# A block-wise attention and a sine-gated MLP in one Trainium2 kernel: the first load goes ahead of an index table, and work units, PSUM banks and a weight load are dealt anew

## The chip, the core and the metric

The kernel runs on one core of a Trainium2 chip. A core has a matrix engine (TensorE, PE in the profile, with weight loads shown as PEld), a vector engine (VectorE, DVE), a scalar engine for functions and copies (ScalarE, ACT), a general engine (GpSimd, POOL) and a queue engine (SyncE, SP). Each takes its own instructions in order. Data comes and goes by 16 DMA engines; a load that converts float32 to bf16 on its way is issued by POOL. The metric is the device time of one execution in microseconds. The median of three runs of the kernel before is 210.96 us (210.64 to 211.02).

## The reference

Two operators in a row. The first is a linear attention over 4 batches, 8 heads, 768 positions and 64 channels with a decay `lam` per head, written in blocks of 64; the second is an MLP on the 3072 x 512 result.

```python
for b in range(nb):                                  # blocks of 64 positions
    intra = einsum('bhic,bhjc->bhij', qb, kb) * Dmask    # lam^(i-j), i >= j
    intra = einsum('bhij,bhjd->bhid', intra, vb)
    inter = einsum('bhid,bhde->bhie', qb * lam_pow, kv_state)
    out[:, :, sl] = intra + inter
    kv_state = lam_block * kv_state + einsum('bhsd,bhse->bhde', kb * rev_pow, vb)
x = out.transpose(0, 2, 1, 3).reshape(3072, 512)
h = x @ w_in                                         # 512 x 2048
g = h + sin(alpha * h)**2 / (alpha + 1e-9)
result = g @ w_out                                   # 2048 x 512
```

## The kernel before, in words

The 768 positions are cut into six chunks of 128 (`NT`), and a chunk holds all four batches, so the MLP works on 512 rows at a time. While PE does the MLP of chunk g, the attention of chunk g+1 is laced into it.

**Loads.** k and q of chunk 0, batch 0, come as float32 from SP and ACT (L81). All others are issued by POOL in program order: `load` (L104, and L101 and L102 where heads are turned by one), `load_w_in` (L89), `load_w_out` (L92). In the program's order they are: k and q of batches 1 to 3, v in two halves, w_in in four quarters (the first in two halves), w_out's first quarter (L544), and then, between POOL's own work on decayed keys (`decay_k`, tile `kdec`, L226) and on the mask table (`mask_table`, L189), the loads of chunk 1 and the other quarters of w_out. Before the first of these loads POOL fills `dist`, a table of i - j (`iota`, L110), from which DVE makes the identity, the triangle and the position columns (L125 to L144).

**Chunk 0** (L499 to L554) has a routine of its own. k and q are turned on PE (`turn`, L265) and copied from PSUM by ACT (L267); `scores1` multiplies them (L290) and DVE applies the decay mask (L294, tile `STm`, from the pool `work`, which has three buffers of it); `outs` multiplies with v (L300) and brings the result to `xt`, by ACT for batch 0 (L304) and with the table `Etab` by DVE for the others (L306). ACT makes `Etab` (L183) and, in `decay_tables` (L155, L178), the tables R128, NE64, R64, L128 and L64; L128 is read by nobody. `spin` (L496) issues products of a constant.

**The MLP.** `hidden(g, f)` makes one of 16 blocks of 128 hidden channels: four products of 128x128 by 128x512 into one PSUM bank (L433), then Sin on ACT (L436) and its square on ACT (L441) or DVE (L449). `finish` adds it to h on DVE (L450, tile `gall`). `project(g, m, part)` is the output product, cut into units of four products (L461); a unit needs four finished blocks and one quarter of w_out. `store` copies a finished output tile (ACT L470, DVE L468). Units stand in a list, `behind`, and `run(n)` issues the next n of them. `units` names the places of a chunk's loop at which one is run, and `own` those at which chunk 1's own units join the list.

**Attention of later chunks.** `turns_pair` and `turn` (or a DMA, L242) turn k and q; `states` makes the products of keys and values (L349), `update` adds them to the decayed state on DVE (L327), and POOL casts it to bf16 (L330); `scores` and `masks` (L366, L373) are the products within a block; `outputs_first` multiplies q with the state (L380), `outputs` adds the part within the block (L408), and `leave` scales the sum into `xt` (L415). For chunk 0 the first state comes from `states1` (L316, L324).

**Order and banks.** The order is written out by hand. The eight PSUM banks are also given out by hand: `bank(name, n)`; a new tile in a bank waits until all readers of the one before it are done. `H0` lists the banks of chunk 0's hidden blocks. Between the chunk-0 loop (L581) and the chunk-1 loop (L674) lies a tail (L605 to L635) in which the attention of chunk 1 is interleaved with ten units.

Of the kernel before, what the change touches and what calls it, by code (L numbers as in the profile page):

```python
# [9 lines left out]
ACTF = mybir.ActivationFunctionType  # L10
# [5 lines left out]
def kernel(  # L16
# [29 lines left out]
    qkp = ctx.enter_context(tc.tile_pool(name="qk", bufs=2))  # L46
    vp = ctx.enter_context(tc.tile_pool(name="vv", bufs=3))
    trp = ctx.enter_context(tc.tile_pool(name="trans", bufs=2))
    work = ctx.enter_context(tc.tile_pool(name="work", bufs=3))
    kdp = ctx.enter_context(tc.tile_pool(name="kdec", bufs=2))  # L50
    kvp = ctx.enter_context(tc.tile_pool(name="kvstate", bufs=2))
    xtp = ctx.enter_context(tc.tile_pool(name="xt", bufs=2))
# [5 lines left out]
    def bank(nm, n, dtype=FP32):  # L58
        return psum.tile([P, 512 if dtype is FP32 else 1024], dtype, name=nm, tag=f"b{n}")
# [35 lines left out]
    def load(t, nm, b0, b1):  # L95
# [7 lines left out]
        else:  # L103
# [2 lines left out]
    new_chunk(0)  # L106
    new_chunk(1)

    dist = consts.tile([P, T], FP32, name="dist")
    nc.gpsimd.iota(out=dist[:], pattern=[[1, T]], base=0, channel_multiplier=-1,  # L110
                   allow_small_or_imprecise_dtypes=True)
    for b in range(1, B):
        for nm in "kq":
            load(0, nm, b, b + 1)
    for b in (0, 2):
# [48 lines left out]
    Etab = consts.tile([P, HP, T], FP32, name="Etab")  # L164
    Eb = Etab[:, :, 0:D].unsqueeze(1).broadcast_to([P, 2, HP, D])
    L64 = consts.tile([P, 2, HP], FP32, name="L64")
    L128 = consts.tile([P, 2, HP], FP32, name="L128")
    later = {}

    def decay_tables():  # L170
        nc.scalar.copy(out=lnlam[:, H:H + 2], in_=lnlam[:, 0:2])
        later["R128"] = powers("R128", 2, lnlam[:], [P, H + 2])
        later["NE64"] = powers("NE64", 3, lnlam[:].rearrange("p (hp hd) -> p hd hp", hd=2), [P, 2, HE])
        later["R64"] = powers("R64", 4, lnlam[:], [P, H + 2])
        for L, n in ((L128, T), (L64, D)):
            for pr in range(2):
                for hd, half in enumerate(HALF):
                    nc.scalar.activation(out=L[half, pr, :], in_=lnlam[half, pr + hd:pr + hd + H - 1:2],  # L178
                                         func=ACTF.Exp, scale=float(n))

    def etab(*cs):
        for c in cs:
# [114 lines left out]
    def outs(t, b, n, eng=None):  # L297
        O = bank("O_ps", n)[:].rearrange("p (c i) -> p c i", c=HP)
        for h in range(H):
            nc.tensor.matmul(out=O[halves(h % 2), h // 2, :], lhsT=vn[t][:, b, h, :], rhs=STm[t, b][:, h % 2, h // 2, :],  # L300
                             start=(h < 2), stop=True, skip_group_check=True)
        x = xt[t][:, :, b * T:(b + 1) * T]
        if eng is nc.scalar:
            nc.scalar.copy(out=x, in_=O)  # L304
        else:
            nc.vector.tensor_tensor(out=x, in0=O, in1=Etab[:], op=ALU.mult)  # L306
# [117 lines left out]
            return V if f in (1, 3, 5, 7, 9, 13) else A  # L424
        return A

    H0 = (0, 1, 2, 3, 5, 6, 7, 0, 1, 2, 5, 0, 1, 2, 0, 1)

    def hidden(g, f, between=None):
        hps = bank("hps", H0[f] if g == 0 else (5, 6, 4)[f] if g == 1 and f < 3 else AB[0] if g == 1 and f == 15 else AB[f + 1] if g == 2 and f < 2 else (1, 0, 2)[(f + 2) % 3] if g == 1 and f > 6 else HB[(16 * g + f + 1) % 3])  # L430
        w = w_in_sb[f // 4]
        for c in range(NDC):
            nc.tensor.matmul(out=hps[:], lhsT=w[:, c, (f % 4) * P:(f % 4 + 1) * P],  # L433
                             rhs=xt[g][:, c, :], start=(c == 0), stop=(c == NDC - 1))
        s_sb = mlps.tile([P, GRP], BF16, name="s_sb")
        nc.scalar.activation(out=s_sb[:], in_=hps[:], func=ACTF.Sin, scale=alpha_sb[:, f:f + 1])  # L436
        if between:
            between()
        s2 = mlps.tile([P, GRP], BF16, name="s2")
        if squarer(g, f) is A:  # L440
            nc.scalar.activation(out=s2[:], in_=s_sb[:], func=ACTF.Square)  # L441
        elif squarer(g, f) is G:
            nc.gpsimd.tensor_tensor(out=s2[:], in0=s_sb[:], in1=s_sb[:], op=ALU.mult)
        hps_of[g, f] = (hps, s_sb, s2)
# [10 lines left out]

    def project(g, m, part):
        if part == 0:
            ops_of[g, m] = bank("ops", (OB, AB[3], 1, OB)[m] if g == 0 else AB[0] if g > NT - 3 and m % 2 else OB)
        ops = ops_of[g, m]
        for f in range(4 * part, 4 * part + 4):  # L460
            nc.tensor.matmul(out=ops[:], lhsT=gall[g][:, f, m * P:(m + 1) * P],  # L461
                             rhs=w_out_sb[part][:, f % 4, :],
                             start=(f == 0), stop=(f == NFC - 1))
# [29 lines left out]
    def spin(n, bk, cols=256):  # L493
        ps = bank("hps", bk)
        for _ in range(n):
            nc.tensor.matmul(out=ps[:, 0:cols], lhsT=fill[:, 0:P], rhs=fill[:, 0:cols], start=True, stop=True)  # L496
# [36 lines left out]
    scores1(0, 3, (4, 5))  # L533
    spin(2, 1)
    outs(0, 0, 3, A)
    outs(0, 1, 1)
    warm = consts.tile([P, 1], FP32, name="warm")
    nc.scalar.activation(out=warm[:], in_=lnlam[:, 0:1], func=ACTF.Sin)
    spin(2, 6)
    outs(0, 2, 2)  # L540
    spin(2, 6)
    outs(0, 3, 0)
    spin(5, 6)
    load_w_out(0)  # L544
    decay_k(0, 0, 2)
    for nm in "kq":
        load(1, nm, 0, 2)
    decay_k(0, 2, 4)
    load(1, "v", 0, 2)
    mask_table()  # L550
    load_w_out(1)
    for nm in "kv":
        load(1, nm, 2, 4)
    decay_k(1, 0, 2)  # L554
# [20 lines left out]
    def run(n):  # L575
        for _ in range(min(n, len(behind))):
            behind.pop(0)()
# [2 lines left out]
                    (1, 3), (2, 3), (3, 0), (3, 1), (3, 2), (3, 3)])  # L580
    for f in range(NFC):  # L581
        hidden(0, f)
        if f in (6, 9):
            states1(0, f // 3 - 2, 4 + 2 * (f == 9))
        if f == 9:
            load_w_out(2)
            load(1, "q", 2, 4)
            load_w_out(3)
        if f in (11, 12):
            run(1)  # L590
        if f == 12:
            turns_pair(1, "k", 0, 6, (A, A))
        if f == 13:
            turn(1, "q", 0, 4, A)
            turn(1, "q", 1, 5, V)
        if f == 14:
            scores(1, (0,), (5, 6))
            masks(1, 0)
        if f == 15:
            states(1, (0,), (4, 2))  # L600
            update(1, 0, 0)
            finish(0, 14)
        if f != 14:
            finish(0, f)
    decay_k(1, 2, 4)  # L605
    load(2, "v", 0, 2)
    update(1, 1, 0)
    run(2)
    turns_pair(1, "k", 2, 0, (A, A))
    outputs_first(1, (0,), (5, 6), A)  # L610
    load(2, "v", 2, 4)
    run(1)
    outputs(1, (0,))
    leave(1, 0, (0,))
    run(1)
    states(1, (1,), (4, 2))
    update(1, 0, 1)
    leave(1, 0, (1,))
    load(2, "k", 0, 2)
    run(2)  # L620
    turn(1, "q", 2, 0, A)
    turn(1, "q", 3, 4, V)
    run(1)
    scores(1, (1,), (0, 5))
    masks(1, 1)
    load(2, "k", 2, 4)
    outputs_first(1, (1,), (6, 4), A)
    update(1, 1, 1)
    load(2, "q", 0, 2)
    load(2, "q", 2, 4)  # L630
    run(1)
    outputs(1, (1,))
    leave(1, 1)
    run(2)
    pair_ready(2, 0)  # L635


# [36 lines left out]
    for g in range(1, NT + 1):  # L674
        if g < NT:
            gall[g] = gbp.tile([P, NFC, GRP], BF16, name="gall")
        at = slots(g) if g + 1 < NT else {}
        fd = feed(g) if g + 1 < NT else {}
        if g + 1 < NT:
            new_xt(g + 1)  # L680
        own = {9: (0, 0), 10: (0, 1), 14: (0, 2)} if g == 1 else {}
        units = [1, 3, 5, 6, 9, 10, 14] if g == 1 else [i for i in range(NFC) if g > 2 or i not in (0, 2, 3)]
        for i in range(NFC):
            if g == NT and not behind:
                break
# [46 lines left out]
```

## Time and profile before

| | |
|---|---|
| median of three runs | 210.96 us |
| the profiled execution | 210.92 us |
| its span (first to last recorded instruction) | 209.1 us |
| granted TensorE clock | 1.0 |
| PE busy | 197.3 us, 94% |
| ACT busy | 144.4 us, 69% |
| DVE busy | 135.3 us, 65% |
| POOL busy | 93.6 us, 45% |
| first product of chunk 0's MLP | 17.31 us |
| first product of chunk 1's MLP | 49.60 us |
| last output copy | 205.83 us |

The tables of the profile are read so. In the chain of waits a line gives start, length, engine and the tile or source line. In a timeline a line gives start, length, engine, line, operation, what is written from what is read, and in brackets the idle time of that engine just before, with what ended it. In a table of stretches a line gives the stretch, its length, each engine's busy time with the number of instructions, the granted clock, the DMA share (mean packets in flight for a DMA engine times the length) and GB/s.

### The profile page before, as it was taken

What the parts mean: (1) busy time and instruction counts of PE and PEld (TensorE: products, weight loads), DVE (VectorE), ACT (ScalarE), POOL (GpSimd) and SP (SyncE); (2) the same over time, 40 slices, a digit from 0 to 9 for tenths busy, and PEclk for the clock granted to TensorE, in tenths of its full rate; (3) what the DMA queues carried; (4) which work ended last, traced back from release to release, by engine and by line L of the source; (5) the groups of instructions that cost most, each with busy time, mean ns of one, the idle gap of its engine ahead of it and who ended that gap; (6) DMA issues with size and microseconds to landing.
All of it is one profiled execution on the core that took longest, in us unless ns stands there. A gap on an engine that the chain in (4) does not pass through costs nothing.

```text
span 209.1 us, 5355 instructions
## 1 busy us (share of the span) xinstructions
PE 197.3 (94%) x2203; PEld 97.7 (47%) x2233; DVE 135.3 (65%) x260; ACT 144.4 (69%) x242; POOL 93.6 (45%) x99
## 2 busy tenths in 40 slices
PE   6679998999989999999999999999999999999993
PEld 2444445554444544445444444445444444444462
DVE  4674997665599878978548978557867544444000
ACT  4699999216988898765776775776675787887121
POOL 8999949897639941998942207002000000000000
PEclk9999999999999999999999999999999999999999
DMA  5999999999999999999999908601101101110212
GB/s 103 155 159 206 205 164 181 182 180 155 159 268 71 147 147 170 91 164 183 142 148 191 183 4 136 168 0 53 50 3 53 50 0 50 52 53 0 100 60 92
DMA packets 98920, 24.47 MB, mean 117 GB/s; under 512 B 91072, under 2 KB 95952, under 8 KB 98896
## 3 DMA queue, kind: packets, MB, share of 16 engines
q0 software_dynamic: 77200, 13.37, 85.2%
q1 hardware_dynamic: 20512, 10.50, 23.8%
q10 hardware_dynamic: 1184, 0.27, 0.6%
q8 instruction: 17, 0.28, 0.5%
q14 instruction: 7, 0.06, 0.1%
HBM read 27.28 MB, written 6.29 MB: 161 GB/s over the span
## 4 chain that ended last, share of the span: by engine, by line
PE 66%; DMA 15%; ACT 5%; POOL 5%; DVE 4%; issue 3%; POOLq 0%; ACTq 0%
PE ops L461 32%; PE hps L433 27%; DMA kn<-in_k_dram 7%; DMA w_out<-in_moe_w_out_dram 5%; DMA qn<-in_q_dram 3%; ACT s_sb L436 2%; DVE S L327 2%; POOL kdec L226 2%; PE hps L485 2%; ACT s L441 2%; PE O_ps L380 2%; DVE gall L450 1%; PE F_ps L366 1%; PE O_ps L408 1%; PE KV_ps L349 1%
## 5 line engine op out<-in xcount | busy, mean ns | idle before, releaser
L450 DVE SCALAR_TENSOR_TENSOR gall<-s,r_sb,hps 128x512 bf16<-128x512 bf16 x96 | 70.8, 744 | 42.1 <-ACT s L441 41.8
L433 PE MATMUL hps<-xt,w_in 128*128 128x512 bf16 x370 | 94.9, 379 | 1.6 <-ACT QKT L282 0.3
L461 PE MATMUL ops<-w_out,gall 128*128 128x512 bf16 x352 | 90.4, 379 | 2.0 <-DMA w_out<-in_moe_w_out_dram 0.7
L436 ACT ACTIVATE s_sb<-hps,alpha_sb 128x512 bf16<-128x512 f32 x96 | 65.4, 685 | 33.6 <-PE hps L433 33.0
L441 ACT ACTIVATE s<-s_sb 128x512 bf16<-128x512 bf16 x90 | 56.7, 630 | 2.9
L433 PEld LDWEIGHTS <-w_in 128*128 128x128 bf16 x384 | 36.6, 98 | 44.0 <-issue 1.5
L461 PEld LDWEIGHTS <-gall 128*128 128x128 bf16 x368 | 35.0, 98 | 41.4 <-issue 1.3
L330 POOL CAST sb<-S 128x512 bf16<-128x512 f32 x20 | 12.2, 617 | 37.5 <-DVE S L327 34.2
L226 POOL TENSOR_TENSOR kdec<-kn,R 128x1024 bf16<-128x1024 bf16 x12 | 22.8, 1908 | 5.2 <-DMA kn<-in_k_dram 4.9
L327 DVE SCALAR_TENSOR_TENSOR S<-S,L,KV_ps 128x128 f32<-128x128 f32 x72 | 20.0, 342 | 0.6 <-PE KV_ps L349 0.6
L415 DVE TENSOR_TENSOR xt<-O_ps,Etab 128x512 bf16<-128x512 f32 x20 | 12.8, 682 | 3.5 <-PE O_ps L408 3.5
L104 POOL DMA_DIRECT2D vn<-in_v_dram x12 | 14.3, 1191 | 0.0
L470 ACT COPY o_sb<-ops 128x512 f32<-128x512 f32 x11 | 6.4, 578 | 10.2 <-PE ops L461 10.2
L373 DVE TENSOR_TENSOR STm<-F_ps,C 128x512 bf16<-128x512 f32 x20 | 12.8, 681 | 0.8 <-PE F_ps L366 0.8
L468 DVE COPY o_sb<-ops 128x512 f32<-128x512 f32 x12 | 8.3, 689 | 4.1 <-PE ops L461 4.1
L267 ACT COPY QKT<-T_ps 128x512 bf16<-128x512 bf16 x10 | 5.7, 586 | 6.4 <-PE T_ps L265 6.4
L398 POOL COPY QKT<-QKT 64x2 bf16<-64x2 bf16 x3 | 0.6, 186 | 19.4 <-PE O_ps L380 11.2
L496 PE MATMUL hps<-fill 128*128 128x256 bf16 (+1 forms) x32 | 7.6, 358 | 1.5 <-DVE fill L123 1.5
L104 POOL DMA_DIRECT2D kn<-in_k_dram x8 | 8.8, 1100 | 0.3 <-issue 0.3
L104 POOL DMA_DIRECT2D qn<-in_q_dram x8 | 8.6, 1077 | 0.0
L380 PEld LDWEIGHTS <-sb 64*64 64x64 bf16 x320 | 4.2, 108 | 4.3 <-issue 4.2
L294 DVE TENSOR_TENSOR STm<-F_ps,C 128x512 bf16<-128x512 f32 x8 | 5.0, 682 | 1.7 <-PE O_ps L300 1.1
(69 smaller groups left out, 109.4 us busy)
## 6 DMA issues: line engine op xcount, KB each, us to landing
out_dram<-o_sb SPq DMA_DIRECT2D x23, 256.0 KB, 2.5
vn<-in_v_dram POOLq DMA_DIRECT2D x12, 256.0 KB, 7.7
w_out<-in_moe_w_out_dram POOLq DMA_DIRECT2D x4, 512.0 KB, 12.5
w_in<-in_moe_w_in_dram POOLq DMA_DIRECT2D x3, 512.0 KB, 12.0
kn<-in_k_dram POOLq DMA_DIRECT2D x5, 256.0 KB, 8.1
qn<-in_q_dram POOLq DMA_DIRECT2D x5, 256.0 KB, 7.8
kn<-in_k_dram POOLq DMA_DIRECT2D x5, 240.0 KB, 8.6
qn<-in_q_dram POOLq DMA_DIRECT2D x5, 240.0 KB, 9.6
```

What stands on the lines that cost most here:

```text
L104: nc.gpsimd.dma_start(out=to, in_=by_head)
L226: nc.gpsimd.tensor_tensor(out=kdec[t][:, b0:b1, :, :], in0=kn[t][:, b0:b1, :, :], in1=R[:, o:o + H].unsqueeze(1).unsqueeze(3).broadcast_to ...
L327: nc.vector.scalar_tensor_tensor(out=S[:, bs, hp, :], in0=old[:, bs, hp, :], scalar=decay[:, pr, hp:hp + 1], in1=ps[:, :, hp, :], op0=ALU. ...
L330: nc.gpsimd.tensor_copy(out=dst[:, bs], in_=S[:, bs])
L373: nc.vector.tensor_tensor(out=st[:, hd], in0=att["F", t, pr, hd], op=ALU.mult, in1=of_mask(C64, t, pr, hd).unsqueeze(1).broadcast_to([P, 2 ...
L380: nc.tensor.matmul(out=att["O", t, pr, blk][halves(h % 2), u, h // 2, :], lhsT=home(t, blk)[halves(half), 2 * pr + m // HP, m % HP, :], rh ...
L415: nc.vector.tensor_tensor(out=xview(t)[:, 2 * pr:2 * pr + 2, blk, :, :], in0=att["O", t, pr, blk], in1=Eb, op=ALU.mult)
L433: nc.tensor.matmul(out=hps[:], lhsT=w[:, c, (f % 4) * P:(f % 4 + 1) * P], rhs=xt[g][:, c, :], start=(c == 0), stop=(c == NDC - 1))
L436: nc.scalar.activation(out=s_sb[:], in_=hps[:], func=ACTF.Sin, scale=alpha_sb[:, f:f + 1])
L441: nc.scalar.activation(out=s2[:], in_=s_sb[:], func=ACTF.Square)
L450: nc.vector.scalar_tensor_tensor(out=gall[g][:, f, :], in0=s2[:], scalar=r_sb[:, f:f + 1], in1=hps[:], op0=ALU.mult, op1=ALU.add)
L461: nc.tensor.matmul(out=ops[:], lhsT=gall[g][:, f, m * P:(m + 1) * P], rhs=w_out_sb[part][:, f % 4, :], start=(f == 0), stop=(f == NFC - 1))
```

## The change

The first load (k of batch 1) is issued before the index table, and q of batch 1 after it. The pool `work` gets a fourth buffer. L128 is dropped, and the tables for blocks of 64 are made after ACT's copy of batch 0. The spins of chunk 0's end are dealt anew (five products in place of nine, most of them ahead of batch 2). The first hidden block is cut by columns into batches 0 to 2 and batch 3. The second quarter of w_out is issued ahead of v of chunk 1. `states1` of the first pair moves from f=6 to f=3. In the tail one unit is run before the states, one after the turned keys, and three in place of two at the end, so that eleven units lie there; chunk 1's loop has six places in place of seven. Banks are renumbered to suit.

```diff
-    work = ctx.enter_context(tc.tile_pool(name="work", bufs=3))
+    work = ctx.enter_context(tc.tile_pool(name="work", bufs=4))
...
+    load(0, "k", 1, 2)
     dist = consts.tile([P, T], FP32, name="dist")
     nc.gpsimd.iota(out=dist[:], pattern=[[1, T]], base=0, channel_multiplier=-1,
                    allow_small_or_imprecise_dtypes=True)
-    for b in range(1, B):
+    load(0, "q", 1, 2)
+    for b in range(2, B):
...
-        for L, n in ((L128, T), (L64, D)):
-            for pr in range(2):
...
-    H0 = (0, 1, 2, 3, 5, 6, 7, 0, 1, 2, 5, 0, 1, 2, 0, 1)
+    H0 = (0, 1, 2, 3, 5, 6, 7, 0, 1, 2, 5, 0, 1, 2, 0, 2)
...
-        for c in range(NDC):
-            nc.tensor.matmul(out=hps[:], lhsT=w[:, c, (f % 4) * P:(f % 4 + 1) * P],
-                             rhs=xt[g][:, c, :], start=(c == 0), stop=(c == NDC - 1))
+        for n0, n1 in ((0, GRP - T), (GRP - T, GRP)) if g + f == 0 else ((0, GRP),):
+            for c in range(NDC):
+                nc.tensor.matmul(out=hps[:, n0:n1], lhsT=w[:, c, (f % 4) * P:(f % 4 + 1) * P],
+                                 rhs=xt[g][:, c, n0:n1], start=(c == 0), stop=(c == NDC - 1))
...
-            ops_of[g, m] = bank("ops", (OB, AB[3], 1, OB)[m] if g == 0 else AB[0] if g > NT - 3 and m % 2 else OB)
+            ops_of[g, m] = bank("ops", (OB, AB[3], 6, OB)[m] if g == 0 else AB[0] if g > NT - 3 and m % 2 else OB)
...
     outs(0, 0, 3, A)
+    decay_tables_64()
     outs(0, 1, 1)
...
-    spin(2, 6)
+    spin(4, 6)
     outs(0, 2, 2)
-    spin(2, 6)
     outs(0, 3, 0)
-    spin(5, 6)
+    spin(1, 6)
...
     decay_k(0, 2, 4)
+    load_w_out(1)
     load(1, "v", 0, 2)
     mask_table()
-    load_w_out(1)
...
-        if f in (6, 9):
-            states1(0, f // 3 - 2, 4 + 2 * (f == 9))
+        if f in (3, 9):
+            states1(0, f // 9, 4 + 2 * (f // 9))
...
         if f == 15:
-            states(1, (0,), (4, 2))
+            run(1)
+            states(1, (0,), (4, 1))
...
-    run(2)
-    turns_pair(1, "k", 2, 0, (A, A))
-    outputs_first(1, (0,), (5, 6), A)
+    run(1)
+    turns_pair(1, "k", 2, 5, (A, A))
+    run(1)
+    outputs_first(1, (0,), (0, 5), A)
     load(2, "v", 2, 4)
     run(1)
     outputs(1, (0,))
     leave(1, 0, (0,))
-    run(1)
-    states(1, (1,), (4, 2))
+    states(1, (1,), (4, 1))
...
-    turn(1, "q", 2, 0, A)
-    turn(1, "q", 3, 4, V)
+    turn(1, "q", 2, 2, A)
+    turn(1, "q", 3, 0, V)
     run(1)
-    scores(1, (1,), (0, 5))
+    scores(1, (1,), (5, 2))
...
-    outputs_first(1, (1,), (6, 4), A)
+    outputs_first(1, (1,), (0, 4), A)
...
     leave(1, 1)
-    run(2)
+    run(3)
...
-        own = {9: (0, 0), 10: (0, 1), 14: (0, 2)} if g == 1 else {}
-        units = [1, 3, 5, 6, 9, 10, 14] if g == 1 else [i for i in range(NFC) if g > 2 or i not in (0, 2, 3)]
+        own = {6: (0, 0), 9: (0, 1), 14: (0, 2)} if g == 1 else {}
+        units = [1, 3, 5, 6, 9, 14] if g == 1 else [i for i in range(NFC) if g > 2 or i not in (0, 2, 3)]
```

More of the change, by code (lines that the diff above doesn't have):

```diff
@@ L166 @@
     L64 = consts.tile([P, 2, HP], FP32, name="L64")
-    L128 = consts.tile([P, 2, HP], FP32, name="L128")
     later = {}
@@ L172, in decay_tables, with decay_tables_64 @@
         later["R128"] = powers("R128", 2, lnlam[:], [P, H + 2])
+    def decay_tables_64():
         later["NE64"] = powers("NE64", 3, lnlam[:].rearrange("p (hp hd) -> p hd hp", hd=2), [P, 2, HE])
         later["R64"] = powers("R64", 4, lnlam[:], [P, H + 2])
-        for L, n in ((L128, T), (L64, D)):
-            for pr in range(2):
-                for hd, half in enumerate(HALF):
-                    nc.scalar.activation(out=L[half, pr, :], in_=lnlam[half, pr + hd:pr + hd + H - 1:2],
-                                         func=ACTF.Exp, scale=float(n))
+        for pr in range(2):
+            for hd, half in enumerate(HALF):
+                nc.scalar.activation(out=L64[half, pr, :], in_=lnlam[half, pr + hd:pr + hd + H - 1:2],
+                                     func=ACTF.Exp, scale=float(D))
     def etab(*cs):
@@ L425, in squarer @@
         return A
-    H0 = (0, 1, 2, 3, 5, 6, 7, 0, 1, 2, 5, 0, 1, 2, 0, 1)
+    H0 = (0, 1, 2, 3, 5, 6, 7, 0, 1, 2, 5, 0, 1, 2, 0, 2)
     def hidden(g, f, between=None):
-        hps = bank("hps", H0[f] if g == 0 else (5, 6, 4)[f] if g == 1 and f < 3 else AB[0] if g == 1 and f == 15 else AB[f + 1] if g == 2 and f < 2 else (1, 0, 2)[(f + 2) % 3] if g == 1 and f > 6 else HB[(16 * g + f + 1) % 3])
+        hps = bank("hps", H0[f] if g == 0 else (5, 7, 4)[f] if g == 1 and f < 3 else AB[0] if g == 1 and f == 15 else AB[f + 1] if g == 2 and f < 2 else (1, 0, 2)[(f + 2) % 3] if g == 1 and f > 6 else HB[(16 * g + f + 1) % 3])
         w = w_in_sb[f // 4]
-        for c in range(NDC):
-            nc.tensor.matmul(out=hps[:], lhsT=w[:, c, (f % 4) * P:(f % 4 + 1) * P],
-                             rhs=xt[g][:, c, :], start=(c == 0), stop=(c == NDC - 1))
+        for n0, n1 in ((0, GRP - T), (GRP - T, GRP)) if g + f == 0 else ((0, GRP),):
+            for c in range(NDC):
+                nc.tensor.matmul(out=hps[:, n0:n1], lhsT=w[:, c, (f % 4) * P:(f % 4 + 1) * P],
+                                 rhs=xt[g][:, c, n0:n1], start=(c == 0), stop=(c == NDC - 1))
         s_sb = mlps.tile([P, GRP], BF16, name="s_sb")
```

## The prediction

> **What bounds it now.** I read the page's busy shares first (PE 94% of the span), then the chain of waits, then the timeline of each stretch, then bytes per stretch. From 49.6 us on, PE goes on almost without a break. So two things can move the end: when PE can begin that stretch, and gaps in it. The chain names the first:
>
> ```profile
> 0.83 0.23 POOL dist L110
> 1.06 0.27 issue
> 1.33 1.08 POOL kn L104
> 2.41 0.89 POOL qn L104
> ...
> 36.03 10.44 DMA w_out<-in_moe_w_out_dram
> 46.47 0.04 issue
> 46.51 0.38 PE ops L461
> ```
>
> The last quarter of w_out lands at 46.47, and PE takes it at 46.51. It is no lone late load. Issue plus time to landing (the tiles' answers) gives: second w_in quarter 10.6 + 10.2 = 20.8; first w_out quarter 12.76 + 15.7 = 28.46; k of chunk 1, batches 0-1, 30.32; second w_out quarter 23.88 + 12.5 = 36.4; k, batches 2-3, 38.0; third w_out quarter 33.45 + 8.8 = 42.25; q, batches 2-3, 43.87. PE is at each within 0.3 us, with one exception (that k pair: turned at 31.30). The timeline shows two of these waits, and POOL issued the loads 9 to 16 us earlier, so their place in line counts and not their issue:
>
> ```profile
> 20.83 0.76 PEld L433 LDWEIGHTS <-w_in 128*128 128x128 bf16 x5 [0.40 <-DMA w_in<-in_moe_w_in_dram]
> 36.42 1.89 PE L461 MATMUL ops<-w_out,gall 128*128 128x512 bf16 x8 [0.50 <-DMA w_out<-in_moe_w_out_dram]
> 42.34 1.89 PE L461 MATMUL ops<-w_out,gall 128*128 128x512 bf16 x7 [0.25 <-DMA w_out<-in_moe_w_out_dram]
> ```
>
> The line never runs dry: 145 to 160 GB/s while it carries q, k, v and 200 to 210 for weights, to 55 us. Only its beginning has room (columns as in the stretches: busy per engine, clock, DMA share, GB/s):
>
> ```profile
> 2.00:3.00 1.00, 1.00 (x4) 0.30 (x3) 0.48 (x4) 0.95 (x1) 1.00 (x2) 1.00 0.26 53
> 3.00:4.00 1.00, 1.00 (x4) 0.32 (x3) 0.00 (x0) 0.04 (x1) 1.00 (x2) 1.00 0.70 155
> 6.00:7.00 1.00, 0.18 (x2) 0.00 (x0) 0.52 (x1) 0.58 (x1) 1.00 (x2) 1.00 2.42 154
> ```
>
> DMA share 0.26 and 0.70 against 2.42 when full: bytes brought into 2 to 4 us shorten all that follows.
>
> **Part by part.** Times are those of the profiled execution (210.92; span 209.1 and 1.82 around it), 0.04 under the median 210.96.
>
> 1. First load ahead of the index table. POOL now runs L110 at 0.83, a gap of 0.27, then k at 1.33. The gap belongs either to the table (k then starts at 0.83: 0.50 earlier) or to the load (1.10: 0.23 earlier). The next load, q, now waits for k and the table: 0.83 + 1.08 + 0.23 + 0.27 = 2.41, as before. Its data landed 5.8 us after issue, so at least 2 us stood in line (a 256 KB v load into an empty line, issued at 63.46, took 4.7) and it loses nothing. The line gains what k can move early: 0 if the two raw loads, in flight until about 6.4, give back what it takes, 0.50 at most. I take 0.4, nearer the upper end because 2 to 4 us was so empty. DVE's work on the table (ten instructions, 1.31 to 2.49) moves about 1.1 later, to 3.6; the first taker is ACT at 5.48, and DVE's next own work is at 4.20. Free; without that cover, up to 1.1 on the first turns.
>
> The ten DVE instructions now lie beside q's issue: 0.90 for a load without them, 1.08 for the one with them. The Trainium skill ("SBUF — State Buffer", section "SBUF: two separate sides") says that VectorE in a two-port mode keeps GpSimd from writing descriptors; the 0.18 agrees. By it q would come 0.18 later, still inside its 2 us in line.
>
> 2. Front. The fourth mask product waited 1.07 for its buffer until O_ps of L300 was done (14.08); with four buffers it can start at about 13.35. The second half of v lands at about 15.25 as before; the spin (0.33) between its two products goes ahead of them. DVE then scales batch 2 at 15.75 and batch 3 at 16.4, done at 17.05 (was 17.16). The first hidden block starts on batches 0-2 at 16.5 instead of 17.31: 4 x 0.16 + 4 x 0.06 (four transposes of 128 columns take 0.23) = 0.88, done at 17.4 instead of 18.17. ACT keeps pace: four L128 instructions go (4 x 0.204), so Sin is loaded 0.8 earlier. That is 0.8 for PE up to f=4, and then PE stands before the w_in quarter of 20.8. Kept: 0. The first states product moves from f=6 to f=3 and lies inside that stand.
>
> 3. w_out ahead of v, and order in the tail. The wait of 0.50 at 36.42 goes. Late next is v: now 32.0 (k, then q at 1.7 per 256 KB) + 2.5 (512 KB at 205) = 34.5 for w_out and 36.2 for v. PE: h of f=15 waits 0.4 for bank 2 (gall of 13, done about 34.65), ends 35.6, its unit 36.4, states just behind v. All that waits for states sits behind it on DVE (four state updates 1.12, then gall 14 and 15), and then POOL's cast (0.62) and kdec (1.90): inter-block products possible at 38.9, kdec at 40.8. PE wants the first at 39.5 (a further 0.4 goes to bank 5, whose two QKT copies end at 39.87) and the second at 41.9. Both hide. PE then stands before the third w_out quarter as now, 42.3. So PE's times against the line are unchanged: 0 kept, 0 lost.
>
> 4. One unit (4 x 0.216 = 0.86) moves ahead of chunk 1, one goes from i=10. PE's sum is the same. States of chunk 2 come 0.86 later relative to the rest, and from there DVE ran without a break from 57.90 to 68.61. That train shifts by 0.86, so h of f=12, which needs bank 2 from f=9's gall, can start at 68.75 (67.83 + 0.86, and its semaphore). It started at 68.74. On the way PE wins 0.42 because the ACT copy of L470 no longer stands before the QKT copies (wait at 62.06), and gives it back at f=12:
>
> ```profile
> 60.76 1.02 PE L433 MATMUL hps<-xt,w_in 128*128 128x512 bf16 x4 [0.28 <-DVE gall L450]
> 62.06 1.02 PE L433 MATMUL hps<-xt,w_in 128*128 128x512 bf16 x4 [0.28 <-ACT QKT L282]
> ```
>
> Bounds: -0.44 if DVE has slack that I don't see, +0.15 if ACT's later block 10 pushes the four x scalings of 70.30. I take 0.
>
> Sum: -0.4 (line) + 0 + 0 + 0: 210.92 - 0.4 = **210.5**.
>
> **Rivals.**
>
> - A, the forecast: the line shifts by 0.2 to 0.5, all else returns to it: 210.4 to 210.7. Chance 0.45.
> - B, the change doesn't do what it says: the line doesn't start earlier. For it: raw loads already moved 270 to 280 GB/s at 4.2 to 5.0, so k's early bytes may only push them back. Against it: share 0.26 and 0.70 before 4.0. Time 210.92 less 0 to 0.2: 210.7 to 210.9. Chance 0.14. The Trainium skill ("DMA: Bandwidth & Descriptors", section "Queues, rings and completion order") says that an engine turns round-robin between its queues by packets, which by itself would make early k packets cost the raw loads turns; the trace of before has no case of it. By that the sum would be 210.9.
> - C, more: the shift is 0.5 and the 0.42 at 62.06 stays won, or the 0.42 at 60.76 goes too: 210.92 - 0.5 - 0.42 = 210.0; 209.9 to 210.4. For it: both waits are in the rows. Against: DVE's unbroken train. Chance 0.27.
> - D, slower: v becomes the late load. Both halves of that swap share 16 engines that finish apart; today no row shows when v landed, only that it was there at 35.48. If it lands 1.2 late, at 37.4, PE stands in order before it, with 0.25 of slack ahead of the k turn (37.8 against 38.06). It decides from 36.6 on. Price 1.2 - 0.25 = 0.95, less 0.4: 211.4 to 211.6. Against it: total bytes ahead of it are the same as those ahead of w_out now. Chance 0.14.
>
> **How the numbers follow.** About 0.2% (0.42) is what a measurement of this kernel can tell from no change, so under 210.54 counts as faster and over 211.38 as slower. A lies across the bound: 0.18 faster, 0.27 same. C is faster (0.27), B the same (0.14), D slower (0.14). Faster 0.45, same 0.41, slower 0.14. Range: C's lower part at 210.0, and upward past B to 211.1, leaving out most of D and a little of C.
>
> **What would show it.** Step 1: k issued at 0.83 to 1.1; third and fourth w_out quarter at PE 0.2 to 0.5 before 42.34 and 46.51. If h of f=0 starts at about 16.5 and the wait on w_in at f=4 grows, step 2 is right; if PE runs on through it, the line came earlier than I think. Step 3: a wait on v in place of the 0.50 on w_out, under 0.3; more is D. Step 4: h of f=12 in chunk 1 starts 22.2 after the fourth w_out quarter is taken (68.74 - 46.51); less is C. The forecast is wrong if w_out's last quarter is no longer what PE meets at its unit, or if chunk 1 has a new wait over 0.4.

## The result, and the profile after

The changed kernel takes 211.97 us (median of six runs, 211.33 to 212.32) against 210.91 for the kernel before (six runs). The ratio is 1.005, with a 95% interval of 1.0033 to 1.0068: slower by 0.5%, where 0.2% faster was the forecast and no more than 211.1 the upper end of its range. The profiled execution took 211.76, with a span of 209.9 (before: 210.92 and 209.1), at a granted clock of 1.0, so 0.84 has to be found.

PE's busy time is unchanged: 197.4 against 197.3. What has grown is time in which PE stands still. The chain of waits says that its cause has another name now. Before, its line by engine read PE 66%, DMA 15%, ACT 5%, POOL 5%, DVE 4%, issue 3%; the line after is

```profile
PE 68%; DVE 10%; ACT 8%; issue 4%; DVEq 0%; ACTq 0%
```

DMA has left the chain: PE no longer meets w_out's last quarter as it lands, it comes behind it. I followed PE from the first load on. First POOL (start, length, engine, line, operation; in brackets the idle time before and what ended it):

```profile
1.24 1.07 POOL L104 DMA_DIRECT2D kn<-in_k_dram  x1 [0.79 <-POOLq L720]
2.39 0.26 POOL L111 IOTA dist<- 128x128 f32 x1
2.58 0.90 POOL L104 DMA_DIRECT2D qn<-in_q_dram  x1
```

k goes out 0.09 earlier than before (1.33), not 0.23 to 0.50, and q 0.18 later. Now the stretches that the prediction called the only room in the line of loads (DMA share and GB/s are the last two columns):

```profile
2.00:3.00 1.00, 1.00 (x4) 0.31 (x3) 0.31 (x4) 0.96 (x1) 0.92 (x3) 1.00 0.24 49
3.00:4.00 1.00, 1.00 (x4) 0.31 (x3) 0.94 (x8) 0.00 (x0) 1.00 (x2) 1.00 0.55 119
6.00:7.00 1.00, 0.58 (x6) 0.34 (x6) 0.47 (x2) 0.49 (x3) 1.00 (x3) 1.00 2.44 155
```

From 3 to 4 us the engines moved 119 GB/s instead of 155. The room was not filled, it grew. From 6 us on the line runs at its old rate, so what is missing there (4 + 36 = 40 KB by 4.0) is not made up: by 46 us POOL's queue has moved 7.22 MB, and 7.26 before.

Then PE in the tail, in its timeline:

```profile
35.47 0.81 PE L436 MATMUL hps<-xt,w_in 128*128 128x512 bf16 x3 [0.32 <-DVE gall L453]
36.33 1.03 PE L464 MATMUL ops<-w_out,gall 128*128 128x512 bf16 x4
37.28 0.45 PE L351 MATMUL KV_ps<-vn,kdec 64*64 64x64 bf16 x32
...
38.70 0.62 PE L281 MATMUL T_ps<-iden,kn 128*128 128x128 bf16 x8
...
42.74 1.90 PE L464 MATMUL ops<-w_out,gall 128*128 128x512 bf16 x7
...
45.88 0.38 PE L368 MATMUL F_ps<-QKT 64*64 64x64 bf16 x23
46.76 0.26 PE L368 MATMUL F_ps<-QKT 64*64 64x64 bf16 x9 [0.50 <-issue]
46.85 0.67 PE L382 MATMUL O_ps<-QKT,sb 64*64 64x64 bf16 x31
47.45 0.82 PE L464 MATMUL ops<-w_out,gall 128*128 128x512 bf16 x2
```

The 0.50 on w_out is gone (36.33 stands without a bracket), as predicted, and the turned k pair is at 38.70 instead of 38.15. The weight load ahead of it shows why:

```profile
38.70 0.39 PEld L281 LDWEIGHTS <-kn 128*128 128x128 bf16 x7 [0.49 <-DMA kn<-in_k_dram]
```

k lands at 38.66 (before: 38.02). The third w_out quarter landed at 42.50, but PE is only there at 42.74 (before: 42.34, waiting). And then comes a stop that no part of the prediction has: in the middle of 32 score products, after the 23rd, PE stands for 0.50 and waits for nothing but "issue". So the last quarter is taken at 47.45 instead of 46.51: **0.94 late, of which about 0.4 came from late data and 0.5 from that stop.** The quarter itself landed at 46.95 (before: 46.47), so without the stop PE would still have been 0.44 late. Behind it nothing more is lost; the span is 0.8 longer.

### The profile page after: what moved, and what is told of

It reads as the page before. It is cut to its first block, busy times and chain, and to the rows that moved or that the text cites. A ratio compares the mean times of both kernels' runs of the same rounds, so it can differ in the third digit from the quotient of the medians.

```text
span 209.9 us, 5351 instructions
## 1 busy us (share of the span) xinstructions
PE 197.4 (94%) x2203; PEld 97.7 (47%) x2233; DVE 136.3 (65%) x260; ACT 143.8 (68%) x238; POOL 93.4 (44%) x99
## 4 chain that ended last, share of the span: by engine, by line
PE 68%; DVE 10%; ACT 8%; issue 4%; DVEq 0%; ACTq 0%
PE ops L464 33%; PE hps L436 27%; ACT s_sb L439 5%; DVE gall L453 5%; DVE S L329 4%; ACT s L444 3%; PE O_ps L382 2%; PE hps L488 2%; PE O_ps L410 1%; DVE s L452 1%; PE KV_ps L351 1%; PE F_ps L368 1%; ACT QKT L284 1%; PE T_ps L281 0%; DVE o_sb L471 0%
## 5 line engine op out<-in xcount | busy, mean ns | idle before, releaser
L436 PE MATMUL hps<-xt,w_in 128*128 128x512 bf16 (+2 forms) x375 | 94.8, 377 | 2.8 <-DVE xt L308 1.0
L436 PEld LDWEIGHTS <-w_in 128*128 128x128 bf16 x388 | 37.1, 98 | 44.7 <-issue 2.4
L375 DVE TENSOR_TENSOR STm<-F_ps,C 128x512 bf16<-128x512 f32 x20 | 12.8, 682 | 1.5 <-PE F_ps L368 1.5
L104 POOL DMA_DIRECT2D qn<-in_q_dram x8 | 8.7, 1082 | 0.0
L101 POOL DMA_DIRECT2D qn<-in_q_dram x5 | 6.2, 1232 | 0.0
```

The costliest lines, as they stand in the source:

```text
L104: nc.gpsimd.dma_start(out=to, in_=by_head)
L375: nc.vector.tensor_tensor(out=st[:, hd], in0=att["F", t, pr, hd], op=ALU.mult, in1=of_mask(C64, t, pr, hd).unsqueeze(1).broadcast_to([P, 2 ...
L436: nc.tensor.matmul(out=hps[:, n0:n1], lhsT=w[:, c, (f % 4) * P:(f % 4 + 1) * P], rhs=xt[g][:, c, n0:n1], start=(c == 0), stop=(c == NDC - 1))
```

## The experiments

All ratios are to the kernel before on the same chip, with 95% intervals. In the diffs "..." stands for lines left out.

### One part at a time

The load first alone, the whole change with the table first again, the tail's order alone, and the whole change without the tail:

```
e1, against before:
+    load(0, "k", 1, 2)
     dist = consts.tile([P, T], FP32, name="dist")
...
+    load(0, "q", 1, 2)
-    for b in range(1, B):
+    for b in range(2, B):
e2, against after: these lines as before
e3, against before: the tail, own, units and the bank numbers of after
e4, against after: the tail, own, units and the bank numbers of before
```

> The kernel before with one edit: the first load (k of batch 1) ahead of the index table, q of batch 1 behind it. Theory 1 (the early load itself delays the start: in the changed kernel's profile the raw k load landed at about 5.4 instead of 5.05, and the first w_in product began 0.31 later): 0.3 to 0.5 slower, 211.2 to 211.4, with k's float32 copy on VectorE longer than 0.43 us. Theory 2 (the loss lies in the tail, the early load is neutral): within 0.1 of the kernel before. My prediction's step 1: 0.4 faster, 210.5.

> The changed kernel with the index table back ahead of all loads. Theory 1: 0.3 to 0.5 faster than the changed kernel, about 211.5, and the first product of the MLP before 17.31. Theory 2: no change against it, about 211.9. If both theories hold a part, 211.5 with a gap left over to 210.9.

> The kernel before with only the tail's edits: units dealt anew (eleven in the tail, six places in chunk 1), banks renumbered; load order, first chunk and w_out's place as before. Theory 1: within 0.2 of the kernel before, 210.9. Theory 2: 0.4 to 0.9 slower, 211.3 to 211.8, with PE idle for about 0.5 within the scores of L366's successor near 46 us, as in the changed kernel.

> The changed kernel with the tail of the kernel before (units, places, banks as before), so: load first, new front, w_out ahead of v, first states product at f=3. Theory 1: as the changed kernel or up to 0.3 less, 211.5 to 212.0. Theory 2: at the kernel before or under it, 210.5 to 210.9.

Measured: e1 1.0014 (1.0 to 1.0027), e2 1.0032 (1.0021 to 1.0042), e3 1.0035 (1.0024 to 1.0045), e4 1.0037 (1.0023 to 1.0051). No part wins and the parts don't simply add. In e1 the line is late as in after (130 GB/s in 3 to 4 us), and the last quarter is taken at 46.73, 0.22 late: the gain of step 1 isn't there, though the interval of the loss begins at none. In e4, v ends the wait in place of w_out: the states start at 37.05 after 1.06 of idle time. In e3 the loss has two places:

```profile
36.39 1.02 PE L461 MATMUL ops<-w_out,gall 128*128 128x512 bf16 x4 [0.45 <-DMA w_out<-in_moe_w_out_dram]
37.35 0.45 PE L349 MATMUL KV_ps<-vn,kdec 64*64 64x64 bf16 x32
...
46.48 0.26 PE L366 MATMUL F_ps<-QKT 64*64 64x64 bf16 x9 [0.33 <-issue]
```

The unit that now stands ahead of the states needs w_out's second quarter, and here v is still loaded first: unit and states wait together, and the states come at 37.35 instead of 35.48. The second place is the stop in the scores, after the same 23rd product as in after. It appears in all three kernels with the new tail (after, e2, e3: 0.50, 0.41, 0.33) and not in the others (before, e1, e4).

### The stop in the scores

Two theories. "Refill": PE's instructions come in transfers of 16 KB, seen as packets of queue q8; PE runs out of them because the next transfer comes too late. In the trace a packet of q8 starts at 44.28 in e2 and e3 and at 44.55 in after; where there is no stop it starts at 42.36 (before), 42.98 (e1) or 43.53 (e4). The stop ended 2.2 to 2.6 after the packet (46.48 in e3, 46.76 in after, 46.88 in e2). "Data": the products wait for something late that the profile doesn't name. In the first case, 24 more PE instructions (12 weight loads and 12 products) far ahead, in PE's idle time of 6 to 7 us, shift the place of the refill, and the stop moves or goes; in the second they change nothing. e8 also deals a third unit of w_out's first quarter ahead of those of the second, so that the unit in front of the states no longer needs the late quarter.

```
e5, against e3:
     turn(0, "k", 0, 4, A)
+    spin(12, 3, 128)
     spin(2, 3)
e8, against e5:
-    queue_units(0, [(0, 0), (1, 0), (0, 1), (1, 1), (2, 0), (2, 1), (0, 2),
+    queue_units(0, [(0, 0), (1, 0), (2, 0), (0, 1), (1, 1), (2, 1), (0, 2),
```

> The tail alone (the kernel before with only the tail's edits, 211.59, whose profile has PE idle for 0.33 within the scores at 46.15) with twelve more constant products of 128 columns at 5.8, where PE stands idle for 1.0: all later PE instructions lie 24 places further on in PE's instruction stream. Theory 'refill' (that idle time is PE waiting for its next instructions: it begins at the same place, about the 953rd instruction, in all three kernels with the new tail, and a 16 KB instruction transfer comes 2.2 ahead of its end): the gap at the 953rd instruction moves or goes, 0.2 to 0.4 faster than the tail alone, 211.2 to 211.4. Rival 'data' (the scores wait for a PSUM bank or a copy): the gap stays before the same product of the scores, 211.6.

> The tail alone with the twelve early products and one more edit: the third unit is (2,0), which needs no second w_out quarter, in place of (0,1). If the tail's loss is the states product standing behind the wait for w_out (0.45 in its profile) plus the refill gap (0.33), nothing of it is left: 210.8 to 211.0, within 0.1 of the kernel before. If the bank waits of the tail (h of f=15, outputs_first) are what costs, 0.3 to 0.5 slower than the kernel before remains.

e5 is 1.0017 (1.0008 to 1.0026) where e3 is 1.0035, so the fills are worth about 0.4 us there (e3 and e5 ran on different chips, so only their ratios can be compared). The packet of q8 starts at 43.72. The timeline shows the scores as one line without a bracket:

```profile
45.85 0.63 PE L366 MATMUL F_ps<-QKT 64*64 64x64 bf16 x32
46.31 0.67 PE L380 MATMUL O_ps<-QKT,sb 64*64 64x64 bf16 x31
46.91 1.04 PE L461 MATMUL ops<-w_out,gall 128*128 128x512 bf16 x4
```

But they take 0.63, and 0.45 before: the stop is still there, shorter and at another product. The same timeline, ended at 45.97, has the first eleven alone:

```profile
45.85 0.28 PE L366 MATMUL F_ps<-QKT 64*64 64x64 bf16 x11
```

From the start of the eleventh product to that of the twelfth it takes 0.18, where the others follow at 0.01 to 0.04. All later runs with the fills have the stop at this place too (e8, e9, e10, e12: 0.33, 0.32, 0.28, 0.31); without them it lies between the 23rd and the 24th (after, e2, e3: 0.69, 0.60, 0.53 from start to start, of which the bracket shows only what lies behind the 23rd product's end, and the profile models the ends of products). So 24 instructions more ahead of it moved the stop forward by exactly 12 products with their 12 weight loads: it keeps its place in PE's stream of instructions. And in all eight kernels with the new tail the products go on 2.2 to 2.6 after the packet of q8 starts. In the nine with the old tail the packet starts 3.0 to 3.7 ahead of the 23rd product, and none of them stops.

Refill holds, data falls: not one load or engine operation of the tail was changed. The Trainium skill ("Runtime: NRT & Kernel Launch", section "Instruction fetch mechanics") says that instructions are refilled in blocks of 16 KiB or 256 instructions, and that crossing such a boundary is mostly hidden. The size of the packets agrees (16 KB each); hidden it is not here, PE stood for 0.33 to 0.50. e8 was 1.0017 (1.0006 to 1.0027): the wait for w_out at 36.39 is gone and the last quarter is taken at 46.67, but the time is that of e5.

### The place of w_out, and the front

```
e6, against before:
+    load_w_out(1)
     load(1, "v", 0, 2)
     mask_table()
-    load_w_out(1)
e7, against before: the fourth buffer, L128, the split tables, the spins, the cut first block and f=3 as in after
```

> The kernel before with one edit: w_out's second quarter issued ahead of v of chunk 1. Theory 'v is the late load': PE waits about 1.0 for v before the states product at 36 (v lands near 36.9 instead of 33.4), k of batches 2-3 lands 0.5 later than 38.0, time 0.5 to 0.9 slower, 211.4 to 211.8. Rival (the change without the tail is slow because of its front): within 0.2 of the kernel before, 210.9. My prediction's step 3 alone, without the reordered tail: a wait of 0.7 on v, half of it made good at the next wait.

> The kernel before with only the front's edits: four buffers, tables split and L128 dropped, spins dealt anew, first hidden block cut, first states product at f=3. Theory 'the line of loads hides the front' (load first alone began the MLP 0.97 later and reached the last w_out quarter only 0.22 later): within 0.15 of the kernel before, 210.75 to 211.05, with the first piece of the first block still waiting for the last x copy, since its instruction stands behind one wait for DVE. Rival (the front costs by itself): 0.3 or more slower.

e6 1.0043 (1.0018 to 1.0068). The wait has changed its owner and grown:

```profile
36.99 0.45 PE L349 MATMUL KV_ps<-vn,kdec 64*64 64x64 bf16 x32 [0.69 <-DMA vn<-in_v_dram]
```

v lands at 36.95, w_out at 35.25, and k of batches 2 and 3 at 38.55 instead of 38.02, although the same 4.12 MB had been moved from 16 to 38 us. So the line isn't slower. The trace has sixteen updates for each load, one for each share, and a load has landed with the last of them. Of that k pair the eighth share landed at 36.61 (before: 36.56) and the fifteenth at 37.66 (37.67); only the last one is late, by 0.53. It is the same with w_out (fifteenth 34.10, last 35.25) and v (35.90, 36.95). The lag isn't the same in every run: in e2, which has w_out ahead of v too, v landed at 36.47 and k at 38.23. Why one share lags is not shown.

e7 is 1.0 (0.9991 to 1.0009): step 2's "kept: 0" is right to 0.1%. The cut of the first block did not start it earlier: its first piece, which needs batches 0 to 2 only, still starts at 17.29 after 1.04 of idle time that the last scaled batch ends (L306); in after it is 17.62 and L308.

### The cures together

If the loss of the change is load first, refill and swap, then taking away the first two by runs must leave little.

```
e9, against e2:    +    spin(12, 3, 128)
e10, against after: +    spin(12, 3, 128)
e12, against e10:
-    load_w_out(1)
     load(1, "v", 0, 2)
     mask_table()
+    load_w_out(1)
```

> The change with the table ahead of the first load again and with 12 early fill products of 128 columns, which move PE's refill of instructions to another place. Theory (the loss of the change is three pieces: load first 0.2 to 0.3, the transfer of w_out ahead of v about 0.3 to 0.4, the refill gap 0.4 to 0.5): no gap inside the scores near 46.5, the run that was 211.46 comes down by 0.3 to 0.4, so 0.2 to 0.4 over before. Rival (the loss is not the refill but the later data alone): as without fills, 0.6 over before, with the scores in one piece or not. A second rival: the fills only move the gap to another place, and nothing is won.

> The whole change with the 12 early fill products. Theory of three pieces: 0.35 to 0.5 under the change, so 0.5 to 0.7 over before; the scores near 46.5 in one piece, k of batches 2 and 3 still waited for at about 38.7. Rival (data alone): as the change, 1.0 over before.

> The whole change with v ahead of the second w_out quarter again (as before) and with the 12 early fill products: what is left of the change is the load first, the front and the tail. Theory: the wait for the second w_out quarter is back (about 0.5 at 36.5), k of batches 2 and 3 lands near 38.2 to 38.3; 0.2 to 0.4 over before, and 0.2 to 0.4 under the change with fills alone. Rival (the place of the w_out quarter is free, its loss in the earlier run came from the wait on a gall buffer at 27.9): the same as the change with fills, 0.5 to 0.7 over before.

| | without the fills | with the fills |
|---|---|---|
| load first | 1.0050, 1.0033 to 1.0068 (after) | 1.0021, 1.0009 to 1.0034 (e10) |
| table first | 1.0032, 1.0021 to 1.0042 (e2) | 1.0009, 1.0 to 1.0019 (e9) |

The fills, which shorten the stop, are worth 0.23 to 0.29%, about 0.5 to 0.6 us; with e3 and e5 that is three pairs. The load first comes out at 0.12 to 0.18%, about 0.25 to 0.4, but here the intervals of both pairs overlap, so its price is only likely. What is left in e9 is 0.2 us (interval 0 to 0.4), with a stop of 0.32 still in its trace.

e12 is a miss: 1.0036 (1.0024 to 1.0048), no better than e10 but probably 0.3 worse (the intervals overlap). Alone (e6) the swap loses 0.9; beside the unit that stands ahead of the states it loses nothing and may win. In e12 PE takes the last w_out quarter at 47.45, 0.79 after its landing, and turns the k pair at 39.09, 0.93 after its landing: in the tail it no longer waits for data, it is late by itself. On its way it waits three times for `gall` (0.31, 0.36 and 0.32, before 27.20, 28.97 and 36.02), where e9 has 0.16 and 0.32 for the last two and nothing for the first. Why, I can't say.

The profiled executions of e9 and e10 (211.55 and 212.35) lie above their medians (210.90 and 211.10); in both the line started late. These are e10's stretches:

```profile
2.00:3.00 1.00, 1.00 (x4) 0.31 (x3) 0.31 (x4) 0.96 (x1) 0.92 (x3) 1.00 0.03 4
3.00:4.00 1.00, 1.00 (x4) 0.31 (x3) 0.94 (x8) 0.00 (x0) 1.00 (x2) 1.00 0.47 101
```

The first data came some 0.5 later (4 GB/s from 2 to 3 us; e9 has 4 and 107), and these executions are 0.65 and 1.25 above their own medians. In e9 the raw k landed 0.56 after e2's, about what its time lost; in e10 it landed 0.43 after after's, which doesn't explain all of its 1.25.

### Why the load first makes the line later

Three candidates: q, now behind the table, goes out 0.18 later; DVE's table work, now at 2.69 to 4.4, lies beside the issue and the first bytes; k's early packets take turns from the raw loads.

```
order of POOL's first work, against before (dist, k, q, ...):
e11   dist, k, idle (an unused table), q, ...
e14   k, q, dist, ...
e15   idle, k, dist, q, ...
e13, against before, behind idf:
+    for _ in range(9):
+        nc.vector.tensor_scalar(out=again[:], in0=dist[:], scalar1=0.0, scalar2=None, op0=ALU.is_ge)
```

> The kernel before with a second, unused index table between the first and the second load: k is issued at 1.33 as before, q at about 2.7 to 2.9 instead of 2.40, and all loads behind it as much later. It takes apart the two causes that could make the line of loads start later when the load goes first. If q's later issue is the cause (0.18 later cost about 0.2): the line is 0.2 to 0.4 later, last w_out quarter taken at 46.7 to 46.9, time 0.2 to 0.4 over before. If the cause is that k's packets then move between those of the raw loads and that the table work on DVE is stretched beside descriptor writing: no change, within 0.1 of before, the last w_out quarter taken at 46.5.

> The kernel before with nine more comparisons of 128x128 on DVE behind the table work, into an unused tile: at 0.15 to 0.22 apiece they keep DVE at work from 2.5 to about 4.0, the stretch in which the load first puts the table work (2.69 to 4.4), while every load is issued as before. If DVE's work at the time of the issue and of the first bytes is what makes the line start later, the bytes of 3 to 4 us fall from 155 GB/s to about 130, the comparisons stretch to 0.4 to 0.6 each, and the time rises by 0.2 to 0.3. If it is the packets of the earlier k load among those of the raw loads, nothing changes: 155 GB/s, within 0.1 of before. A third case: the comparisons themselves stretch, so that DVE comes late to its copy at 4.2, and the line is as before: 0 to 0.1.

> The kernel before with two loads, k and q, ahead of the index table: k at 1.24, q at about 2.3, the table at about 3.2, its work on DVE from about 3.5 to 5. If q's place behind the table or DVE's work beside its issue is the cause of the later line, the bytes of 3 to 4 us come back to 150 GB/s or more, though the line's next issue is again beside DVE; time 0 to 0.2 over before. If the early k packets are the cause, as with one load first or worse: 130 GB/s or less in 3 to 4 us, and 0.2 to 0.5 over before. In both cases DVE comes later to the raw casts (about 5.6 instead of 5.08), which the line's waits hide.

> The load first as in the change, but behind an unused index table: POOL runs the unused table at 0.83, k at 1.33, the real table at about 2.4, q at about 2.6. From the run with q later it differs in one thing only, which of the two tables DVE's work waits for, so that work lies at 2.7 to 4.4 as in the load first. If the raw loads are slowed because k goes out at 1.24 with nothing on POOL ahead of it, they now move as before (some 300 packets of raw k in 3.5 to 4.0, 155 GB/s in 3 to 4) and the time is within 0.1 of before. If they are slowed because the table's work lies late on DVE, they move as with the load first (170 to 210 packets, 120 to 130 GB/s) and the time is 0.2 to 0.3 over before.

e11, with q at 2.61, is 0.9997 (0.9978 to 1.0016) and moves 159 GB/s in 3 to 4: q's issue is innocent. e13 is 1.0075 (1.0062 to 1.0089), but by another way than the one tested. The line is as before:

```profile
3.00:4.00 1.00, 1.00 (x4) 0.32 (x3) 0.93 (x3) 0.04 (x1) 1.00 (x2) 1.00 0.71 158
...
8.00:9.00 1.00, 0.76 (x6) 0.70 (x7) 1.00 (x3) 0.11 (x1) 1.00 (x2) 0.50 2.43 155
```

The nine comparisons took 3.81 instead of 1.4 to 2.0 (nine times 0.16 to 0.22), so DVE came to its first cast at 7.00 instead of 5.08, PE stood from 5.0 to 8.2 and its granted clock (the column ahead of the DMA share) fell to 0.50. The front is covered by the line only so far. DVE's work doesn't slow the line.

e14 moves 121 GB/s in 3 to 4, so its line is as late as with one load first, and it takes the last w_out quarter at 46.69, 0.18 late; its time, 1.0005 (0.9991 to 1.0019), can't be told from no change. For the third candidate the packets of each queue decide it. From 2 to 4 us the queue of POOL's loads (q0) has none at all, in any run; its first come at 4.36 to 4.50 (5.05 and 5.09 in the late executions of e10 and e9). Here are the rows of e1 and of e15 for 3.5 to 4.0 (queue, kind, packets, MB, share; q1 brings raw k, q10 raw q):

```profile
q1 hardware_dynamic: 211, 0.05, 47.0%
q10 hardware_dynamic: 94, 0.02, 18.0%
```

```profile
q1 hardware_dynamic: 294, 0.08, 65.6%
q10 hardware_dynamic: 84, 0.02, 17.0%
```

So packets of k can't have taken turns in the stretch that slowed, and the third candidate falls as well. The slow ones are the raw loads themselves: 173 to 214 packets of raw k in that half microsecond where the load stands first on POOL (e14, after, e12, e1, e4; 230 in e10, whose data began late), and 252 to 313 where any table, even an unused one, stands ahead of it. e15 is 1.0 (0.9985 to 1.0014), with 153 GB/s in 3 to 4: k at 1.33, q at 2.61, the real table's work as late on DVE as in e1, and nothing lost. **What slows the raw loads is to issue k at 1.24 as POOL's first own work rather than at 1.33 behind an iota.** Whether the 0.09 or the place counts, and by what way it slows loads whose issues on SP (1.25) and ACT (1.19) lie beside it, stays open.

What was lost there stays lost. These are POOL's queue up to 46 us (packets, MB, share) in before, e15, e1 and e14, which issue all their loads in the same order:

```profile
q0 software_dynamic: 28965, 7.26, 177.4%
q0 software_dynamic: 28922, 7.26, 176.5%
q0 software_dynamic: 28807, 7.24, 176.3%
q0 software_dynamic: 28785, 7.23, 175.7%
```

The 20 to 30 KB that e1 and e14 lack are 0.1 to 0.15 us of a line of 200 GB/s. That is an estimate from these rows, and it is less than the 0.25 to 0.4 that the pairs above come out at. Where the rest of that price lies, if it is there, is not shown.

## Why the prediction was wrong

The sum was -0.4 for the line and three times 0; measured is +1.06. Step 1's gain did not come, step 3's 0 was about 0.4 of late data, and a term of about 0.5 was in no step.

**Step 1, the gain.** "The line gains what k can move early: 0 ... 0.50 at most. I take 0.4." It gained nothing: e1 is 0.3 slower (0 to 0.6), e14 0.1 (-0.2 to 0.4), and the two pairs come out at 0.25 to 0.4. So a loss is likely, and its size is not settled. Two things failed in it. The gap of 0.27 was given to the table or to the load; POOL starts at 1.24 for a third reason, its own queue (0.79 after POOLq). And the room in 2 to 4 us could not be filled by this load: no packet of POOL's queue moves before 4.36, some 3 us after the issue. Rival B named the right failure, a line that doesn't start earlier, but had no loss in it; its way, turns between queues, was wrong, and so was the use of the rule on turns from the Trainium skill ("DMA: Bandwidth & Descriptors", section "Queues, rings and completion order"): no packet of k moved in the half microsecond that slowed. The 0.18 read from 0.90 and 1.08 as a price of DVE's work was wrong too: in after k's issue takes 1.07 with no table work beside it and q's 0.90 with it. It is DVE that stretches (the triangle 0.22 before, 0.58 in after), and e15 shows that this costs nothing. That q "loses nothing" was wrong as well: it landed at 8.60 instead of 8.16, and not for its later issue (in e11 it was issued at 2.61 and landed at 8.24).

**Step 2, right in its sum.** Kept 0; e7 is 1.0. But the block began at 17.62 in after instead of 16.5, because the cut did not free its first piece. So the states product at f=3 did not lie inside the stand before the w_in quarter, as forecast: the quarter landed at 20.86 and PE came there at 21.17. e7 shows that such lateness is hidden there: its states come at 36.26 instead of 35.48, and it takes the last w_out quarter at 46.48 all the same.

**Step 3, the size of v's and k's landings.** It was forecast that v lands at 36.2, k as before, and that "PE then stands before the third w_out quarter as now, 42.3". v landed at 37.06 and k at 38.66, and PE came to the third quarter at 42.74, late by 0.40. The term that was too small is the time of w_out and v in line. The forecast has 5.9 from the landing of k of batches 0 and 1 to that of v (30.32 to 36.2); it was 6.7 in after and e4 and 6.8 in e6, but 5.9 in e2 and 6.0 and 6.1 in e10 and e9. So the size taken is one that occurs, but the forecast went by the mean rate alone, and a load lands with its last share (in e6 v's last share came 1.05 behind its fifteenth). Rival D is right that v comes late, beyond its bound of 36.6, and wrong on what follows: in after PE does not stand before v, because the unit ahead of the states keeps it until 37.28. The wait came one load later, at the k turn (38.70). Nor is that wait the data's alone: PE was behind already, with the scores at 34.70 instead of 34.13, and could have begun the k turn no earlier than about 38.53 (its unit at 37.66, and 0.87 from there to the turn, as in e9). What this part costs inside the whole change isn't settled apart from its tail: alone it loses 0.9 (e6), and with the new tail e10 is about 0.3 faster than e12, which is without it.

**The term that was missing.** The stop of 0.50 for PE's instructions is in no part and no rival. The page of before has the instruction queue (q8) but no wait on it; the same products ran unbroken at 45.46. The reordered tail is where it comes from: there the packet of q8 starts only 1.5 to 2.2 ahead of the product behind which PE stops.

**Step 4, right in its sum.** Its own test was that h of f=12 starts 22.2 after the last w_out quarter is taken: 69.66 - 47.45 = 22.21, as before (22.23). Chunk 1 has no new wait over 0.28. The 0.42 that the step gives the wait at 62.06 is 0.28 in the row shown there; from start to start it is 0.44 (62.06 - 60.76 - 0.86).

**What bounds it.** That PE is pinned to w_out's last quarter was right for before, e1, e11, e14 and e15, which take it within 0.15 of its landing, and for e7 (46.48, landed at 46.39), which is why e7 shows nothing. It was wrong to take it for after: there PE comes 0.50 behind that landing, and then every wait in the tail reaches the end.

## What to carry to other kernels

Room in a table of stretches is not room for every load: look at when the queue's own packets begin, some 3 us after the issue here, before counting on it. Where PE follows a line of loads with under 0.3 us of slack, a swap of two loads can move the landings behind them as well, so price each of them at its next user, and leave room for the last share of a load. A long unrolled stream of instructions is refilled on the way; after any change of order look for idle time put down to "issue" in the middle of one group of products, and try a dozen instructions more or fewer in idle time ahead of it. Then measure the length of the whole group again: a stop can lose its bracket in the timeline and still be there.

## What the runs showed of the hardware that was not expected

- PE can run out of instructions in the middle of a kernel, and gets them 2.2 to 2.6 us after a 16 KB packet of its queue starts (eight traces); it stood for 0.33 to 0.50. 24 more PE instructions some 40 us earlier moved the stop by 12 products and shortened it, from 0.53 to 0.18 between two starts in e5 against e3. Why the new order asks for the transfer later stays open.
- A load issued 0.09 earlier, as POOL's first own work, made the raw loads of other queues slower: 119 to 130 GB/s in 3 to 4 us instead of 155 (after, e1, e4, e12, e14). An unused iota of 0.23 ahead of it cured that (e15: 153).
- Fifteen of a load's sixteen shares can be on time and the last one 0.5 late (k in e6: fifteenth share 37.66 and 37.67 before, last 38.55 and 38.02).
- With PE idle from 5.0 to 8.2 the granted clock fell to 0.50 in the stretches from 8 to 11 us (e13).
- Comparisons of 128x128 on DVE take 0.16 to 0.22 before 2.5 us, and 0.42 on average from 2.4 to 6.2 (e13), beside POOL's issues.
